# mLSTM cell and GELU feed-forward on one core: k and q of the later chunks copied into one piece in DRAM, their blocks loaded in 4 transfers

## The chip, the cores and the metric

One core of one Trainium2 chip. The metric is the time of one execution in device microseconds (us), as the median of several runs. Engines: PE (matrix multiply), PEld (its weight loads, which overlap PE), DVE (vector), ACT (activations), POOL (GpSimd), and SP, whose queue (SPq) issues every transfer of this kernel in program order.

## The reference

An mLSTM cell over batch 4, 8 heads, 768 steps and head size 40, and behind it a feed-forward layer on its output x (3072 tokens of 320 values).

```python
for t in range(S):
    m_new = np.maximum(f_gate[:, :, t] + m, i_gate[:, :, t])
    f_stab, i_stab = np.exp(f_gate[:, :, t] + m - m_new), np.exp(i_gate[:, :, t] - m_new)
    C = f_stab * C + i_stab * (v_t outer k_t);  n = f_stab * n + i_stab * k_t;  m = m_new
    y[:, :, t] = sigmoid(o_gate[:, :, t]) * (C q_t) / max(|n . q_t|, 1)
x = y.transpose(0, 2, 1, 3).reshape(3072, 320)
out = gelu(x @ moe_w_in) @ moe_w_out          # 320 -> 2048 -> 320
```

## The kernel before

The 768 steps are cut into 6 chunks of 128. Each chunk of each of the 4 batches is one unit n = 4c + b, in which the recurrence is written as matrix products: scores k times q for all heads, weighted by exponentials of the gates, times v, and a carried state per batch. After a chunk's cell comes its feed-forward part for 512 tokens: an upward product (`up`, three f32r products of high and low parts of x and of the weights, tiles `x_hi`, `x_lo`, `x_all`), GELU into the tile `g`, and a downward product in seven partial products (`down_steps`).

The program order is written by hand. `FRONT` plays the cells of chunks 0 and 1 and the unpacking of the weights. Then, for c = 1 to 5, `up` of chunk c is played, and after it the string `DOWN`, which mixes the downward products of chunk c (each `F` is one of 14 steps) with the cell of chunk c + 1. Inside `up`, the first two entries `K0 Q0` and `K1 Q1` of that next cell are already played. The letters that matter here, in the order of `DOWN` (`... F F`-steps between them left out): `M1 M0` masks on POOL; `L3` loads the blocks of the last batch; `S0 C0 h0` scores, state reads and state updates of batches 0 and 1; `B3` loads the gate rows of batch 3 into part of `g`; `K2 Q2 K3 Q3` transposes; `V0` ... `V3` values; `M2 M3` masks; `W3` exponentials; `D3` weighs v of batch 3 on POOL (tile `vw`, line 497); `S2 C2 h2` the same as `S0 C0 h0` for batches 2 and 3; `X`, `R` transposes and splits of x; `j` loads the blocks of the first batch of the chunk after.

For chunks 2 to 5, k and q come transposed. A block buffer has 128 partitions: row 64 i + d holds k (i = 0) or q (i = 1). `load_blocks` (lines 153 to 163, the transfer is line 160) fills it so that DVE's 32 by 32 transposes (line 458) give kT and qT: for k and q, for columns 0 to 31 and 32 to 39 of the head, and for 4 groups of 32 steps there is one transfer each, 16 per batch. Batches 0 to 2 of a chunk share one buffer (`blocks`), so each set is loaded after the transposes of the set before. Batch 3 uses half of `g`, the hidden tile of chunk c: `load_last` clears rows 32 to 63 and 96 to 127 on POOL (line 447) and loads 16 transfers, when the downward product no longer needs that part of `g`.

On SP's queue behind the 16 transfers of `L3` stand, in this order: the gate rows of batch 3 (line 177), k and v for batch 3 (line 148, four half transfers, which also wait until batch 0's k and v have been read), a `W` (line 180), k and v of the next unit (line 150). PE's state update of batches 2 and 3 (line 592) takes `vw` and `kb`.

Of the kernel before, what the change touches and what calls it, by code (L numbers as in the profile page):

```python
# [9 lines left out]
F32 = mybir.dt.float32  # L10
F32R = mybir.dt.float32r
# [5 lines left out]
P = 128  # L17
# [22 lines left out]
def kernel(  # L40
# [16 lines left out]
    nc = tc.nc  # L57

    B, H, S, D = q.shape
    L = P  # L60
    NCH = S // L
# [7 lines left out]
    TG = B * L  # L69
    R = P // 2  # L70
    NX = 2
# [12 lines left out]
    dram = ctx.enter_context(tc.tile_pool(name="dram", bufs=1, space=bass.MemoryType.DRAM))  # L84
# [36 lines left out]
    beyond = gates.tile([P, L], BF16, name="beyond")  # L121
    f_sb = gates.tile([BH, NCH, L], F32, name="f_sb")
    i_sb = gates.tile([BH, NCH, L], F32, name="i_sb")
    M_d = dram.tile([NCH - 1, BH, L], F32, name="M_d")
    swapped_d = [dram.tile([P, n, BH], F32, name=f"swapped{n}") for n in (NCH - 2, NCH - 3)]

# [12 lines left out]
    def load(n, first=0, end=4):  # L139
# [4 lines left out]
        for src, dst in ((q, qb), (k, kb), (v, vb), (o_gate, None))[first:end]:  # L144
            if dst and swapped(c, b):
                x, to = src[b, :, c * L:(c + 1) * L, :].rearrange("h p d -> p h d"), dst[turn_of(n)][:, :, 0:D]
                for i in range(2):
# [2 lines left out]
            nc.sync.dma_start(out=dst[turn_of(n)][:, :, 0:D] if dst else out_of(n),  # L150
                              in_=src[b, :, c * L:(c + 1) * L, :].rearrange("h p d -> p h d"))

    def load_blocks(n, to):

        c, b = divmod(n, B)
        for i, src in enumerate((k, q)):
            for d, w in ((0, 32), (32, D - 32)):
                for g in range(4):
                    t = c * L + 32 * g
                    nc.sync.dma_start(out=to[64 * i + d:64 * i + d + 32, :, 32 * g:32 * g + w],  # L160
                                      in_=src[b, :, t:t + 32, d:d + w].rearrange("h t d -> t h d"))
# [116 lines left out]
    def decays_last(g0, g1):  # L278
        g = slice(g0, g1)
        pd = ps_tr.tile([P, g1 - g0, BH], F32, name="pd", tag="tr")  # L280
        nc.tensor.matmul(pd.rearrange("p c n -> p (c n)"), last, gT[:, g].rearrange("p c n -> p (c n)"),
                         start=True, stop=True)
        by_half = pd.rearrange("p c (n two) -> p c n two", two=2)
        for hip in range(2):
            nc.vector.tensor_copy(out=dec[halves[hip], g], in_=by_half[halves[hip], :, :, hip])
# [109 lines left out]
    class Cell:  # L395
# [46 lines left out]

        def load_last(self, b):

            self.by_block = self.before.t[:, 0:HF, 0:P]
            for r in (32, 96):
                nc.gpsimd.memset(self.by_block[r:r + 32], 0.0)  # L447
            load_blocks(self.c * B + b, self.by_block)
# [14 lines left out]
        def turn_q(self, b):  # L463
            self.turn_half(b, 1)
            if b < B - 2:
                load_blocks(self.c * B + b + 1, by_block)
            if self.c < NCH - 1 and b < B - 1:
                self.weigh_values(b)
# [210 lines left out]

        def split_x(self, b):  # L680
            px, t = self.px.pop(b), slice(b * L, (b + 1) * L)
            hi = parts["x"][:, :, t]
            nc.vector.scalar_tensor_tensor(out=parts["x_lo"][:, :, t], in0=px, scalar=-1.0 / BASE, in1=hi, op0=OP.mult, op1=OP.add)
            nc.vector.tensor_tensor(out=parts["x_all"][:, :, t], in0=px, in1=hi, op=OP.subtract)


    HF, HT, HD = NF // 2, TG // 2, DM // 2
# [9 lines left out]
    w_sums, parts, fars, w_hi, w_lo, w_mid = [], {}, [], [], [], {}  # L697
    T = {1: lambda j: w_sums[0][:, j, :], 2: lambda j: w_sums[1][:, j, :], 3: Bm[0][1]}

    def products_begin():  # L700

        gate_ctx.close()
        pool = ctx.enter_context(tc.tile_pool(name="parts", bufs=1))
        w_sums.extend(pool.tile([P, HF, HD], F32, name=f"w_sums{n}") for n in range(2))
        for name in ("x_lo", "x_all"):
            parts[name] = pool.tile([P, NX + 1, TG], F32R, name=name)
        fars.extend([pool])

    def split_weight():
        i = len(w_lo)  # L710
        if i in (0, 3, 5, 8):
            two = shared([P, NX, 2, WP // 2], F32R, "w_in_hi")
            w_hi.extend([two[:, 0], two[:, 1]])
        elif i == 2:
            two = shared([P, 2, 2, WP // 2], F32R, "w_rest_hi")
            w_hi.append(two[:, 0])
            rest_two.append(two[:, 1])
        elif i == 7:
            w_hi.append(rest_two[0])
        w = w_all[i]  # L720
        nc.scalar.activation(out=w_hi[i], in_=w, func=AF.Copy, scale=PART * 2.0 ** -12)
        w_lo.append(w_f(F32R, "w_in_lo"))
        nc.vector.scalar_tensor_tensor(out=w_lo[i], in0=w_hi[i], scalar=-BASE * 2.0 ** 12, in1=w, op0=OP.mult, op1=OP.add)
# [3 lines left out]
    def join_weight(i):  # L727
        w_mid[i] = raw.tile([P, 2, WP // 2], F32R, name="w_in_mid", tag="pow") if i % 5 in (1, 4) else w_f(F32R, "w_mid")
        nc.vector.tensor_tensor(out=w_mid[i], in0=w_hi[i], in1=w_lo[i], op=OP.add)  # L729
# [22 lines left out]
    def hidden_sums(g, f0, f1):  # L752

        (a11, a21), (_, a22) = [[g.t[:, HF * e + f0:HF * e + f1, HT * h:HT * (h + 1)] for h in range(2)]
                                for e in range(2)]
        s1, s2 = [t[f0 // (HF // 2)][:, f0 % (HF // 2):f0 % (HF // 2) + f1 - f0, :] for t in (g.s1, g.s2)]
        nc.vector.tensor_tensor(out=s1, in0=a21, in1=a22, op=OP.add)  # L757
        nc.vector.tensor_tensor(out=s2, in0=s1, in1=a11, op=OP.subtract)
        nc.vector.tensor_tensor(out=a21, in0=a11, in1=a21, op=OP.subtract)  # L759
# [44 lines left out]
    def up(g, sums_too, turns):  # L804

        def split_to(i):
            while len(w_lo) <= i:
                split_weight()

        def pair(f, ahead):  # L810

            at = [f // 2 * 5 + f % 2 * 3 + x for x in range(NX)]
            split_to(at[1])
            for i in at:
                if i not in w_mid:
                    join_weight(i)
            pus = [[pool.tile([P, TG], F32, name="pu", tag=tag) for e in range(2)]
                   for pool, tag in (((ps_h, "h"), (ps_mm, "a")), ((ps_tr, "tr"), (ps_mm, "b")))[f % 2]]
            ahead()
            mid = [w_mid.pop(i) for i in at]  # L820
            for n, (w, x) in enumerate((([w_hi[i] for i in at], parts["x"]), ([w_lo[i] for i in at], parts["x_lo"]), (mid, parts["x_all"]))):
                for i in range(2):
                    for e in range(2):
                        for k in range(NX):
                            nc.tensor.matmul(pus[i][e], w[k][:, e, i * P:(i + 1) * P], x[:, k, :],  # L825
                                             start=(n == 0 and k == 0), stop=False, skip_group_check=True)
            return pus

        def rest(u, banks, order):
            mid = w_mid.pop(5 * u + 2)  # L830
            for i in order:
                pu = banks[i]
                for n, (w, x) in enumerate(((w_hi[5 * u + 2], parts["x"]), (w_lo[5 * u + 2], parts["x_lo"]), (mid, parts["x_all"]))):
                    for e in range(2):
                        r = halves[e]
                        nc.tensor.matmul(pu[e], w[r, i // 2, i % 2 * P:(i % 2 + 1) * P], x[r, NX, :], start=False,  # L836
                                         stop=(n == 2), skip_group_check=True)

        def out(i, e, pu):
            nc.scalar.activation(out=g.t[:, HF * e + i, :], in_=pu[e], func=AF.Gelu, scale=4097.0)  # L840

        b0 = pair(0, lambda: split_to(4))
        b1 = pair(1, lambda: join_weight(2))
        for step in turns[:1]:
            step()
        rest(0, b0 + b1, (0, 1, 2, 3))
        split_to(6)
        join_weight(5)
        join_weight(6)
        for i, pu in enumerate(b0 + b1):  # L850
            for e in range(2):
                out(i, e, pu)
        for step in sums_too[:5]:
            step()
        b2 = pair(2, lambda: split_to(9))
        hidden_sums(g, 0, 2)
        b3 = pair(3, lambda: (hidden_sums(g, 2, 4), join_weight(7)))
        for step in turns[1:] + sums_too[5:]:
            step()
        rest(1, b2 + b3, (2, 3, 0, 1))  # L860
        for i, e in ((2, 0), (2, 1), (3, 0), (0, 0), (1, 0), (3, 1), (0, 1), (1, 1)):
            out(4 + i, e, (b2 + b3)[i])
        hidden_sums(g, HF - 2, HF)
        hidden_sums(g, HF - 4, HF - 2)
# [100 lines left out]
    def cell_steps(c, letters, before=None):  # L965
# [11 lines left out]
                 d=lambda: decays_last(0, 1), q=lambda: decays_last(1, NCH - 1), r=halves_out, p=halves_back,  # L977
# [5 lines left out]
    for c in range(1, NCH):  # L983
        g, later, steps = Hidden(True), [], {}
# [38 lines left out]
```

## Time and profile before

| | |
|---|---|
| median of 3 runs | 488.13 us (486.6 to 488.46) |
| the profiled execution | 486.33 us, of which the span of the trace is 484.5 us |
| busy: PE / PEld / DVE / ACT / POOL | 471.9 / 408.0 / 338.0 / 244.0 / 76.7 us |
| PE's granted clock, mean | 0.996 |
| moved by DMA | 44.58 MB in 170429 packets, 156448 of them under 512 B |
| transfers issued on line 160 | 256 (192 into `blocks`, 64 into `g`) |
| loop c = 1 to 5: first matmul of `up` | about 129.4, 202.7, 278.7, 351.8 and 422.0 us |

The page comes from one execution, the traced one; its span and the 1.8 us around it make its own time. A stage's limit is read from the idle time of PE in that stage and from what ended it. "A <- B" names the instruction that waited and the one that came last before it.

### The profile page before, as it was taken

What the parts mean: (1) busy time and instruction counts of PE and PEld (TensorE: products, weight loads), DVE (VectorE), ACT (ScalarE), POOL (GpSimd) and SP (SyncE); (2) the same over time, 40 slices, a digit from 0 to 9 for tenths busy, and PEclk for the clock granted to TensorE, in tenths of its full rate; (3) what the DMA queues carried; (4) which work ended last, traced back from release to release, by engine and by line L of the source; (5) the groups of instructions that cost most, each with busy time, mean ns of one, the idle gap of its engine ahead of it and who ended that gap; (6) DMA issues with size and microseconds to landing.
All of it is one profiled execution on the core that took longest, in us unless ns stands there. A gap on an engine that the chain in (4) does not pass through costs nothing.

```text
span 484.5 us, 13245 instructions
## 1 busy us (share of the span) xinstructions
PE 471.9 (97%) x5380; PEld 408.0 (84%) x5380; DVE 338.0 (70%) x726; ACT 244.0 (50%) x521; POOL 76.7 (16%) x120
## 2 busy tenths in 40 slices
PE   8899999999999989999998999999999999999997
PEld 7787888777777979977988977888977899977997
DVE  7899699797879978656687555596755587624321
ACT  6977999844632953221963203774303784211300
POOL 3002200000020322500324500125400113100000
PEclk9999999999999999999998999999999999999999
DMA  9997955379320365651363751245751350100001
GB/s 178 189 226 175 220 138 147 90 190 213 105 29 8 38 136 108 112 107 13 33 141 77 127 106 17 34 87 130 136 107 17 33 95 4 38 20 0 1 1 54
DMA packets 170429, 44.58 MB, mean 92 GB/s; under 512 B 156448, under 2 KB 163904, under 8 KB 170368
## 3 DMA queue, kind: packets, MB, share of 16 engines
q1 hardware_dynamic: 170368, 43.73, 45.5%
q8 instruction: 42, 0.69, 0.6%
q14 instruction: 19, 0.16, 0.1%
HBM read 39.58 MB, written 4.13 MB: 90 GB/s over the span
## 4 chain that ended last, share of the span: by engine, by line
PE 67%; issue 12%; DVE 8%; SPq 4%; DMA 3%; ACT 2%; POOL 2%; DVEq 0%; POOLq 0%; ACTq 0%
PE po L900 22%; PE pu L825 16%; PE po L877 7%; PE pu L770 6%; PE pu L836 4%; PE ph L625 3%; SPq L160 2%; PE px L665 2%; PE pu L776 2%; PE ps L510 1%; SPq L150 1%; ACT g L840 1%; DMA g<-M_d 1%; DVE qT L458 1%; PE pf L548 1%
## 5 line engine op out<-in xcount | busy, mean ns | idle before, releaser
L840 ACT ACTIVATE g<-pu 128x512 f32<-128x512 f32 x80 | 40.8, 616 | 107.7 <-PE pu L836 107.6
L900 PE MATMUL po<-w_out,g 128*128 128x160 f32 x640 | 92.7, 301 | 0.0
L900 PEld LDWEIGHTS po<-w_out,g 128*128 128x128 f32 x640 | 87.9, 190 | 2.3 <-ACT g L840 1.8
L900 PE MATMUL po<-w_sums,sums 128*128 128x160 f32 x320 | 48.5, 309 | 0.0
L900 PEld LDWEIGHTS po<-w_sums,sums 128*128 128x128 f32 x320 | 45.4, 195 | 0.6
L825 PE MATMUL pu<-x_hi,w_in_hi 128*128 128x512 f32 x160 | 41.4, 400 | 0.0
L825 PE MATMUL pu<-x_lo,w_in_lo 128*128 128x512 f32 x160 | 40.6, 396 | 0.0
L435 ACT ACTIVATE W<-W,aT 128x128 f32<-128x128 f32 x128 | 38.7, 388 | 0.4
L825 PEld LDWEIGHTS pu<-x_hi,w_in_hi 128*128 128x128 f32 x160 | 29.4, 188 | 8.1 <-ACT g L840 1.9
L825 PEld LDWEIGHTS pu<-x_lo,w_in_lo 128*128 128x128 f32 x160 | 30.1, 188 | 7.2
L877 PE MATMUL po<-w_out,g 128*128 128x320 f32 x128 | 35.2, 433 | 0.0
L729 DVE TENSOR_TENSOR w_in_mid<-w_in_hi,w_in_lo 128x512 fp32r<-128x512 f32 x20 | 13.8, 688 | 29.5 <-PE pu L825 29.5
L877 PEld LDWEIGHTS po<-w_out,g 128*128 128x128 f32 x128 | 24.0, 190 | 9.6
L825 PE MATMUL pu<-x_all,w_mid 128*128 128x512 f32 x80 | 31.6, 395 | 0.0
L825 PE MATMUL pu<-x_all,w_in_mid 128*128 128x512 f32 x80 | 31.6, 395 | 0.0
L757 DVE TENSOR_TENSOR sums<-g 128x512 f32<-128x512 f32 x20 | 13.8, 688 | 25.5 <-ACT g L840 25.5
L913 DVE TENSOR_TENSOR o_sb<-po,o_sb 128x320 f32<-128x320 f32 (+1 forms) x27 | 12.5, 464 | 24.3 <-PE po L900 20.3
L409 POOL TENSOR_SCALAR_AFFINE_SELECT W<-W 128x1024 f32<-128x1024 f32 (+2 forms) x20 | 20.5, 1027 | 54.2 <-DMA W<-M_d 47.4
L770 PE MATMUL pu<-first_x,w_in 128*128 128x256 f32 x128 | 29.1, 382 | 0.0
L447 POOL MEMSET g<- 32x1024 f32 x8 | 7.6, 945 | 131.5 <-DVE g L759 94.9
L770 PEld LDWEIGHTS pu<-first_x,w_in 128*128 128x128 f32 x128 | 23.8, 190 | 3.5 <-DVE w_in L377 0.4
L532 DVE TENSOR_TENSOR W<-ps,W 128x256 f32<-128x256 f32 (+1 forms) x48 | 18.0, 415 | 11.1 <-PE ps L526 9.8
(185 smaller groups left out, 899.5 us busy)
## 6 DMA issues: line engine op xcount, KB each, us to landing
W<-M_d SPq DMA_DIRECT2D x16, 512.0 KB, 5.3
bits<-in_moe_w_in_dram SPq DMA_DIRECT2D x20, 256.0 KB, 4.4
bits<-in_moe_w_out_dram SPq DMA_DIRECT2D x16, 320.0 KB, 3.2
ob<-in_o_gate_dram SPq DMA_DIRECT2D x24, 160.0 KB, 4.0
out_dram<-o_sb SPq DMA_DIRECT2D x24, 160.0 KB, 1.9
vb<-in_v_dram SPq DMA_DIRECT2D x14, 160.0 KB, 5.2
kb<-in_k_dram SPq DMA_DIRECT2D x14, 160.0 KB, 4.9
g<-M_d SPq DMA_DIRECT2D x4, 512.0 KB, 4.8
```

Of the source, the lines that this page charges most:

```text
L409: nc.gpsimd.affine_select(out=x, in_=x, compare_op=OP.is_ge, fill=1.0e30, base=base, pattern=[[0, H], [1, x.shape[2]]], channel_multiplier=-1)
L435: nc.scalar.activation(out=W[n][:, h, :], in_=src, func=AF.Exp, scale=-1.0, bias=aT[:, self.c, r:r + 1])
L532: nc.vector.tensor_tensor(out=w[r, :, t], in0=ps[i][hip][r, :, t], in1=w[r, :, t], op=OP.mult)
L625: nc.tensor.matmul(ph[r, h, :], Pm[:, h, r], vb[turn_of(n)][:, h, :], start=True, stop=True)
L729: nc.vector.tensor_tensor(out=w_mid[i], in0=w_hi[i], in1=w_lo[i], op=OP.add)
L757: nc.vector.tensor_tensor(out=s1, in0=a21, in1=a22, op=OP.add)
L770: nc.tensor.matmul(banks[-1][e][:, i - i0, :], in_tile(i, x)[:, e, i % 2 * P:(i % 2 + 1) * P], first_x[:, x, t0:t1], start=(x == 0 and i = ...
L825: nc.tensor.matmul(pus[i][e], w[k][:, e, i * P:(i + 1) * P], x[:, k, :], start=(n == 0 and k == 0), stop=False, skip_group_check=True)
L836: nc.tensor.matmul(pu[e], w[r, i // 2, i % 2 * P:(i % 2 + 1) * P], x[r, NX, :], start=False, stop=(n == 2), skip_group_check=True)
L840: nc.scalar.activation(out=g.t[:, HF * e + i, :], in_=pu[e], func=AF.Gelu, scale=4097.0)
L877: nc.tensor.matmul(po[b], g.t[:, f, b * L:(b + 1) * L], w_out[:, f, :], start=(f == 0), stop=(f == NF - 1))
L900: nc.tensor.matmul(bank[at][:, i, :], lhs(j, t), rhs(j), start=(first and i == 0 and j == 0), stop=(i == n - 1 and j == HF - 1), skip_grou ...
```

## The change

- Eight DRAM tiles `kq_d` are added, for k and q of chunks 2 to 5, each of 4 batches x (8 heads x 128 steps) x 40 values. `copy_chunk` copies k and q of a chunk into them, DRAM to DRAM, one transfer of 160 KB for each batch and each of k and q, with rows of 1280 bytes.
- `copy_chunk(2)` stands at the start of `up` of c = 1 and copies batches 2 and 3 only (4 transfers). `copy_chunk(c + 2)` stands in `up` of c = 1, 2 and 3 after `K1 Q1` and copies all 4 batches (8 transfers).
- `load_blocks` of units n > 9 reads the copy. Heads and groups of steps are one dimension there, so a set takes 4 transfers instead of 16. Units 8 and 9 are loaded as before.
- The last batch's blocks no longer lie in `g` but in a tile `blocks3` that shares the buffer of `x_lo`. `x_lo` is made anew for each chunk at its first split.

```diff
+    kq_d = [[dram.tile([B, H * L, D], F32, name=f"{x}{c}_d") for x in "kq"] for c in range(2, NCH)]
...
+    def copy_chunk(c):
+
+        for b in range(B) if c > 2 else range(2, B):
+            for to, src in zip(kq_d[c - 2], (k, q)):
+                for x, y in ((src[b, :, c * L:(c + 1) * L, :], to[b]),):
+                    nc.sync.dma_start(out=y.rearrange("(h x t) d -> x h (t d)", h=H, x=16),
+                                        in_=x.rearrange("h (x t) d -> x h (t d)", x=16))
+
     def load_blocks(n, to):
...
             for d, w in ((0, 32), (32, D - 32)):
+                if n > 2 * B + 1:
+                    nc.sync.dma_start(out=to[64 * i + d:64 * i + d + 32].rearrange("t h (g w) -> t (h g) w", w=32)[:, :, 0:w],
+                                      in_=kq_d[c - 2][i][b, :, d:d + w].rearrange("(x t) d -> t x d", t=32))
+                    continue
                 for g in range(4):
...
         def load_last(self, b):
-            self.by_block = self.before.t[:, 0:HF, 0:P]
+            self.by_block = fars[0].tile([P, H, P], F32, name="blocks3", tag="x_lo", bufs=1)
...
         def split_x(self, b):
             px, t = self.px.pop(b), slice(b * L, (b + 1) * L)
+            if b == 0:
+                parts["x_lo"] = fars[0].tile([P, NX + 1, TG], F32R, name="x_lo", tag="x_lo", bufs=1)
...
-        for name in ("x_lo", "x_all"):
-            parts[name] = pool.tile([P, NX + 1, TG], F32R, name=name)
+        parts["x_all"] = pool.tile([P, NX + 1, TG], F32R, name="x_all")
...
+        if c == 1:
+            copy_chunk(2)
         b0 = pair(0, lambda: split_to(4))
...
         for step in turns[1:] + sums_too[5:]:
             step()
+        if c + 2 < NCH:
+            copy_chunk(c + 2)
         rest(1, b2 + b3, (2, 3, 0, 1))
```

## The prediction

> **What bounds the kernel now.** I read the page first, then PE's timeline around each `DOWN`, then for each gap the engine named as its releaser, and last SP's queue. The page says that PE is the bound:
>
> ```profile
> PE 471.9 (97%) x5380; PEld 408.0 (84%) x5380; DVE 338.0 (70%) x726; ACT 244.0 (50%) x521; POOL 76.7 (16%) x120
> ```
>
> The change does not touch a matmul, so it can only act through PE's 12.6 us of idle time (484.5 less 471.9), or through a slower clock after idle time. PE's timeline in the `DOWN` of c = 2 (start, length, instruction, then the idle time before it) has the largest piece:
>
> ```profile
> 253.37 0.51 PE L592 MATMUL pf<-vw,kb 128*40 128x41 f32 x16
> 254.55 0.31 PE L592 MATMUL pf<-vw,kb 128*40 128x41 f32 x5 [0.68 <-POOL vw L497]
> 256.18 0.52 PE L592 MATMUL pf<-vw,kb 128*40 128x41 f32 x11 [1.32 <-issue]
> 256.63 6.14 PE L900 MATMUL po<-w_sums,sums 128*128 128x160 f32 x32
> ```
>
> PE waits at `h2` for the weighed v of batch 3. The last line is 32 matmuls that take 4.61 us in the other chunks: 1.53 us more. The table by microsecond says why (the granted clock is the third number from the end):
>
> ```profile
> 256.00:257.00 1.00, 0.82 (x12) 0.74 (x13) 0.94 (x3) 0.00 (x0) 1.00 (x2) 0.68 0.04 8
> 258.00:259.00 1.00, 1.00 (x6) 1.00 (x5) 0.97 (x5) 0.98 (x2) 0.00 (x0) 0.50 0.00 0
> 260.00:261.00 1.00, 1.00 (x10) 1.00 (x9) 0.99 (x2) 0.09 (x1) 0.83 (x1) 1.00 0.00 0
> ```
>
> After the two gaps the clock is at half for some 3.4 us. What POOL waited for before that `vw`, and what SP's queue did then:
>
> ```profile
> 251.14 1.81 POOL L409 TENSOR_SCALAR_AFFINE_SELECT g<-g 64x1024 f32<-64x1024 f32 x2 [8.03 <-DMA g<-M_d]
> 253.76 0.73 POOL L497 TENSOR_TENSOR vw<-vb,ewT 128x328 f32<-128x328 f32 x1 [0.81 <-DMA vb<-in_v_dram]
> ```
> ```profile
> 236.72 4.82 SPq L160 DMA_DIRECT2D g<-in_k_dram  x8
> 241.58 5.06 SPq L160 DMA_DIRECT2D g<-in_q_dram  x8
> 246.74 0.40 SPq L177 DMA_DIRECT2D g<-M_d  x1
> 247.26 1.29 SPq L148 DMA_DIRECT2D kb<-in_k_dram  x2
> 248.95 1.27 SPq L148 DMA_DIRECT2D vb<-in_v_dram  x2
> ```
>
> SP spends 236.72 to 246.7 on the 16 transfers of `L3`; gate rows and v of batch 3 stand behind them. So issue time on SP reaches PE. The other `DOWN`s have the same gap, shorter: 0.87 us before line 592 at 330.75 (c = 3), 0.23 us at 181.65 (c = 1), none for c = 4, whose cell updates no state. c = 1 also has one wait for a block itself:
>
> ```profile
> 177.02 1.45 DVE L458 STREAM_TRANSPOSE qT<-g 64x512 f32<-64x512 f32 x2 [0.47 <-DMA g<-in_q_dram]
> ```
>
> **Removed issues.** Units 10 to 23 are 14 sets; 12 fewer transfers each make 168 issues at 0.449 us (the median of line 160's rows), 75 us of SP's queue. 28 copies at about 0.45 us put 12.6 us back. Most of this lies beside other work; what counts is `L3` (9.9 us in c = 2) and the set at `K1 Q1` before it (227.52 to 236.37).
>
> **Does a set also land faster?** The packets do not change: 4096 of 128 or 32 bytes. Between 211 and 221 us only one set runs, and the DMA share of its five 2 us rows is 0.26, 0.40, 0.38, 0.42, 0.15, together 3.2 us of full work for 7.7 us of issuing. So the DMA engines are under half used and the issue is the limit: 4 issues (1.8 to 2.4 us), 3.2 us on the DMA engines and the 2 us that a small transfer takes to land give 5 to 6 us instead of about 10. [...]
>
> **The copies.** No row shows a DRAM to DRAM transfer. Below: 160 KB at the 292 GB/s that the busiest microsecond shows (253 to 254) is 0.55 us of all 16 DMA engines. Above: the same bytes first read and then written, each at the 155 GB/s of a `W` (512 KB in 5.3 us of which 2 are landing), is 2.1 us. I take 0.8 us, near the lower end, since both sides have long rows like the weights' loads (2560 bytes, 283 GB/s between 104 and 108 us). They read inputs and write tiles that nobody holds, so they wait for nothing; each is used 20 us or more later. Behind them on SP stand only `L3` and what follows. `copy_chunk(2)` is 4 issues after 133 us, where SP's next transfer starts at 136.77 when DVE frees `blocks`; it costs nothing while 4 x 0.45 fits those 3.8 us, and 1 or 2 us of a block load with slack otherwise.
>
> **The new buffer.** `L3` waited for `g`, free after DVE's line 759 (236.57). It now waits for PE's last `x_lo` matmul, 231.25 by its row in `rest`. POOL's two memsets (1.95 us) go from 236.87 to about 231.3. Behind them on POOL is the state decay of `h0`, which waits for PE anyway. The `x_lo` written at `R0` must wait for the last transposes of `blocks3`; they are earlier on DVE itself, so this costs nothing.
>
> **The new schedule of c = 2**, from 227.52: 4 issues to 229.6, 8 copies to about 234, `L3` to about 236. `g` rows are free at 236.6, so the gate rows are issued at 236.6 instead of 246.74. The DMA engines have 3.2 + 8 x 0.8 + 3.2 = 12.8 us of work from 228 on, done at 241; the gate rows land by about 244, with `blocks3` at about 242, before DVE's `K3` at 247.5. k and v of batch 3 now wait for `V0`, whose matmuls end at 242.3: issued to 244.9, landed at about 249 (median 4.2 us), `vw` at 249.7. PE wants it at 253.9, so there are some 4 us of slack. c = 1 and c = 3 give the same by their own rows: `vw` at about 176 against 181.4, and at 326 against 329.9.
>
> **Sum.** c = 1: 0.47 + 0.23 = 0.7 us. c = 2: 0.68 + 1.32 + 1.53 = 3.5 us. c = 3: 0.87 us. Together 5.1 us, 486.33 to 481.2 for the profiled execution. The median stands 1.8 us above that one; 488.13 less 5.1 is 483.0. The doubtful part is the 1.32 us "issue": the trace names no cause, and it falls where the DMA share is 1.21 and 0.74. Its bounds are 0 (it stays, and the half clock with it: 2.85 us less gain) and the whole; I take the whole, since c = 1 and c = 3 run the same instructions without it. What stays: `S2` waits 0.31 us for DVE's transposes in c = 2 and 3, where DVE is busy without a break. The half clock follows two gaps of 2.0 us together, and I tie it to them. [...]
>
> **Rivals.** (1) Only the named waits go; the 1.32 us and the half clock stay or fall elsewhere, for the DMA engines are as full as before: 0.7 + 0.68 + 0.87 = 2.25 us, 485.9. For it: nothing in the trace ties them to `vw`. Against: the neighbouring chunks have neither. (2) Nothing reaches PE: gate rows and v come early, but DVE (no break from 237.65 to 250.9) and the next waits take the time back: 488. Against: after `h2` PE has two `F` steps ready, and c = 4, which lacks the wait, runs on with 0.18 us idle. (3) Slower, by the copies alone: they hold the DMA engines ahead of `L3`. `K3` at 247.5 is late once 229.6 + 8r + 3.2 + 2 passes 247.5, that is at r = 1.6 us a copy. At r = 2.1 it is 4.1 us late in three chunks, and the idle time brings the half clock, 1.5 us each: 3 x 5.6 = 17 us. The 5.1 us of waits on `vw` and the block would lie inside these, so 12 are new: 488 + 12 = 500. For it: no row shows such a transfer. Against: stores of 160 KB land in 1.9 us, so writing DRAM is quick.
>
> **How the numbers follow.** This kernel's runs differ by 0.4%, so 0.5% (2.4 us) is about what a measurement can tell from no change. Chances: the forecast 0.50 (482 to 485.5), rival 1 0.20 (485 to 487), rival 2 0.12 (487 to 489.5), rival 3 and its milder forms 0.18. Faster by over 0.5% (below 485.7): the forecast and a fifth of rival 1, 0.54. Same: 0.28. Slower: 0.18. The range goes from 481.5, somewhat under the forecast's sum, to 490.5, where the slow copies begin.
>
> **What would show it.** Right: line 160 has 88 transfers, the gate rows of c = 2 issue near 237, line 592 shows no wait on `vw` in c = 1 to 3, and the clock stays at 1.00 after 250 us. Wrong: copies that take over 1.6 us each, so that DVE's `K3` waits for `blocks3`; or PE's gaps of the same size at another line.

## The result, and the profile after

| | before | after |
|---|---|---|
| median | 488.29 us (486.6 to 490.11, 4 runs) | 480.66 us (479.91 to 481.03, 4 runs) |
| the profiled execution | 486.33 us, span 484.5 | 480.80 us, span 479.0 |
| PE's mean granted clock | 0.996 | 1.000 |
| busy PE | 471.9 us | 468.2 us |

The ratio is 0.9841, 95% interval 0.9803 to 0.9879. The change makes the kernel 7.6 us faster by the medians and 5.5 us by the two traced executions. The forecast was 483.0 us with a range from 481.5, so the result lies 0.8 us below the range.

From the page after, PE's busy time, and further down the queue that will matter in the last experiments (packets, MB, share of 16 DMA engines):

```profile
PE 468.2 (98%) x5380; PEld 405.0 (85%) x5380; DVE 338.9 (71%) x726; ACT 244.1 (51%) x521; POOL 78.3 (16%) x120
...
q8 instruction: 42, 0.69, 0.6%
```

SP's queue in the `DOWN` of c = 2 (start, length, transfer; line 159 is the copy, 168 the short block load, 190 the gate rows, 149 k and v of the last batch):

```profile
229.29 1.08 SPq L159 DMA_DIRECT2D k_d<-in_k_dram  x1
230.42 0.59 SPq L159 DMA_DIRECT2D q_d<-in_q_dram  x1
...
235.50 1.14 SPq L168 DMA_DIRECT2D blocks<-k_d  x2
236.69 1.65 SPq L168 DMA_DIRECT2D blocks<-q_d  x2
238.51 1.44 SPq L190 DMA_DIRECT2D g<-M_d  x1
240.62 1.32 SPq L149 DMA_DIRECT2D kb<-in_k_dram  x2
242.03 2.48 SPq L149 DMA_DIRECT2D vb<-in_v_dram  x2
```

`L3` now takes 235.50 to 238.3 instead of 236.72 to 246.7, and the gate rows are issued at 238.51 instead of 246.74. POOL follows, and so does PE (its timeline at `h2` of c = 2):

```profile
243.53 1.81 POOL L422 TENSOR_SCALAR_AFFINE_SELECT g<-g 64x1024 f32<-64x1024 f32 x2 [1.08 <-DMA g<-M_d]
246.65 0.74 POOL L510 TENSOR_TENSOR vw<-vb,ewT 128x328 f32<-128x328 f32 x1 [1.31 <-DMA vb<-in_v_dram]
```
```profile
252.71 0.61 PE L605 MATMUL pf<-vw,kb 128*40 128x41 f32 x21
253.87 0.43 PE L605 MATMUL pf<-vw,kb 128*40 128x41 f32 x11 [0.55 <-issue]
254.23 4.61 PE L918 MATMUL po<-w_sums,sums 128*128 128x160 f32 x32
```

`vw` of batch 3 is ready at 247.4, PE wants it at 253.2, and no `h2` waits for it any more. The 32 matmuls behind `h2` take 4.61 us (6.14 before) at a granted clock of 1.00, so the half clock is gone too. One piece stays: an idle time of 0.55 us that the trace gives no releaser for ("issue"), behind the same 21st matmul of 32 as before. The DMA engines are done earlier too, at 250 instead of 255.8 (share of the 16 engines next to last; the kernel before has 1.21 and 0.74 in 254 to 256):

```profile
249.00:250.00 1.00, 1.00 (x9) 0.43 (x7) 0.97 (x2) 0.67 (x2) 0.00 (x0) 1.00 0.96 101
250.00:251.00 1.00, 0.69 (x33) 0.69 (x34) 0.26 (x1) 1.00 (x1) 0.00 (x0) 1.00 0.02 4
```

The loops, from the first matmul of one `up` to the next, show where the 5.5 us lie:

| | start to c = 1 | c = 1 | c = 2 | c = 3 | c = 4 | c = 5 |
|---|---|---|---|---|---|---|
| before | 128.95 | 73.74 | 76.03 | 73.05 | 70.19 | 62.57 |
| after | 129.20 | 72.85 | 72.74 | 71.95 | 69.70 | 62.54 |
| gained | -0.25 | 0.89 | 3.29 | 1.10 | 0.49 | 0.03 |
| predicted | 0 | 0.70 | 3.53 | 0.87 | 0 | 0 |

(The first `up` of the kernel before starts at 128.95; the "about 129.4" of the table ahead of the prediction is 0.45 us late.)

### The profile page after: what moved, and what is told of

Same layout as the page of the kernel before. It is cut to its first block, busy times and chain, and to the rows that moved or that the text cites. A ratio compares the mean times of both kernels' runs of the same rounds, so it can differ in the third digit from the quotient of the medians.

```text
span 479.0 us, 13005 instructions
## 1 busy us (share of the span) xinstructions
PE 468.2 (98%) x5380; PEld 405.0 (85%) x5380; DVE 338.9 (71%) x726; ACT 244.1 (51%) x521; POOL 78.3 (16%) x120
## 4 chain that ended last, share of the span: by engine, by line
PE 82%; DVE 8%; DMA 5%; SPq 2%; issue 1%; ACT 1%; POOL 0%; DVEq 0%; POOLq 0%
PE po L918 27%; PE pu L839 22%; PE po L895 7%; PE pu L784 6%; PE pu L850 6%; PE ph L638 3%; PE ps L539 2%; DVE qT L471 2%; PE px L678 2%; PE pu L790 2%; DMA g<-M_d 2%; PE pf L594 1%; DVE kT L471 1%; PE ps L523 1%; SPq L151 1%
## 5 line engine op out<-in xcount | busy, mean ns | idle before, releaser
L918 PE MATMUL po<-w_sums,sums 128*128 128x160 f32 x320 | 47.0, 303 | 0.0
L918 PEld LDWEIGHTS po<-w_sums,sums 128*128 128x128 f32 x320 | 43.9, 190 | 0.6
L422 POOL TENSOR_SCALAR_AFFINE_SELECT W<-W 128x1024 f32<-128x1024 f32 (+2 forms) x20 | 21.5, 1078 | 54.6 <-DMA W<-M_d 47.9
L667 ACT COPY y_rest<-ob 128x128 f32<-128x128 f32 x16 | 4.8, 298 | 40.7 <-DVE ob L660 38.7
L460 POOL MEMSET blocks<- 32x1024 f32 x8 | 7.6, 945 | 108.5 <-PE pu L850 108.3
```

Of the source, the lines that this page charges most:

```text
L422: nc.gpsimd.affine_select(out=x, in_=x, compare_op=OP.is_ge, fill=1.0e30, base=base, pattern=[[0, H], [1, x.shape[2]]], channel_multiplier=-1)
L918: nc.tensor.matmul(bank[at][:, i, :], lhs(j, t), rhs(j), start=(first and i == 0 and j == 0), stop=(i == n - 1 and j == HF - 1), skip_grou ...
```

## The experiments

**How much the kernel before differs from itself.** `e1_before_again` is the kernel before, unchanged.

> The kernel before, unchanged, to see how its executions differ. The traced execution of before (486.33 us) lost 5.5 us to that of after, the medians 7.6. Theory A: the executions of before differ by their count of half-clock stretches of about 3.4 us, each 1.5 to 1.7 us long in time and 0.0035 in the mean granted clock; so the times spread from 486 to 490 and the longer ones show the lower clock (0.993 or less against 0.996). Rival B: the waits of PE for v of batch 3 differ in length from one execution to the next, as transfers land earlier or later; then the times spread as much, the clock stays the same, and a second trace shows the gaps of line 592 at other lengths with one half-clock stretch or none.

Measured: 488.85 us median (485.42 to 490.89), ratio 0.9999 (0.9964 to 1.0035). The spread goes with the clock: executions with a mean clock of 1.000 took 485.4 to 488.6 us, those at 0.992 or 0.993 took 489.5 to 490.9. The clock is not all of it: at 1.000 they still differ by 3.2 us, as the rival has it. Over all 78 executions of the kernel before that have their clock on record, 12 of `e1` and 66 beside the other runs (the stretch of half clock in the trace of the kernel before is 3.41 us long, and one of that length lowers the mean by 0.0035):

| half-clock stretches, from the mean clock | 0 | 1 | 2 | 3 | 4 | 5 |
|---|---|---|---|---|---|---|
| executions | 17 | 30 | 19 | 9 | 2 | 1 |
| median, us | 486.3 | 488.8 | 489.9 | 490.8 | 493.7 | 492.0 |

A straight line through all of them rises by 1.5 us for each stretch. The trace of `e1` has the waits of the one before, but another split at c = 2:

```profile
255.86 0.31 PE L592 MATMUL pf<-vw,kb 128*40 128x41 f32 x5 [0.34 <-POOL vw L497]
258.36 0.43 PE L592 MATMUL pf<-vw,kb 128*40 128x41 f32 x11 [2.20 <-issue]
```

So the traced execution of the kernel before, with one stretch and 486.33 us, was faster than all 30 with one stretch in the table (486.6 to 491.3); it is not a plain offset below the median.

**Which part of the change does it.** Three kernels have one part each. `e2_buffer_only` is the kernel before with the last batch's blocks in the buffer of `x_lo`, still in 16 transfers and without copies:

```diff
-            self.by_block = self.before.t[:, 0:HF, 0:P]
+            self.by_block = fars[0].tile([P, H, P], F32, name="blocks3", tag="x_lo", bufs=1)
```

> Only the second part of the change: the last batch's blocks lie in the buffer of x_lo, and every set is still loaded with 16 transfers from the inputs, with no copies. The queue of SP reaches the set of the last batch at 236.4 instead of 236.7 in the second loop, 163.0 instead of 164.2 in the first, 311.3 instead of 312.7 in the third. Theory: issue time on SP is what counts, so the gate rows and v of batch 3 come only 0.3 to 1.4 us earlier: 0.3 to 0.9 us less wait in loops 1 and 3, the half clock of loop 2 stays; 1 to 2 us faster than before, 486 to 487. Rival: the wait for g is what held the set back, and the new buffer alone gives most of the gain: 482 to 483.

Measured: 487.27 us (485.52 to 489.42), ratio 0.9967 (0.9935 to 0.9999). That is 1.5 us less than the kernel before beside it (488.77), the size that the theory gave, though the interval all but reaches 1. In its trace the only half-clock stretch lies at 15 us and none in c = 2, and at `h2` of c = 2 PE has no wait on `vw` at all, but a longer unnamed gap:

```profile
255.56 0.61 PE L592 MATMUL pf<-vw,kb 128*40 128x41 f32 x21
258.99 0.43 PE L592 MATMUL pf<-vw,kb 128*40 128x41 f32 x11 [2.82 <-issue]
```

`e3_copies_rest` has the copies and the short loads for batches 0 to 2, but batch 3 stays in `g` with 16 transfers:

```diff
-                if n > 2 * B + 1:
+                if n > 2 * B + 1 and b < B - 1:
```

> The copies and the 4-transfer loads for batches 0 to 2 alone; the last batch's blocks stay in g and are loaded with 16 transfers from the inputs. Theory: the set of the last batch still starts when g is free (236.6 in the second loop) and still takes 9 to 10 us of SP, so gate rows and v of batch 3 come as in before, and the copies are only work that nobody waits for: 487 to 489, no change. Rival: the issue time saved on the other sets is worth something by itself (sends, gates, the next k and v come earlier): 484 to 486.

Measured: 489.53 us (488.09 to 491.08), ratio 1.0008 (0.998 to 1.0036), mean clock 0.989 to 0.996. It saves 120 of the 168 issues and gains nothing. SP's queue and PE at c = 2, where again no wait on `vw` is left, and the unnamed gap is the longest of all:

```profile
237.63 4.88 SPq L173 DMA_DIRECT2D g<-in_k_dram  x8
242.56 4.91 SPq L173 DMA_DIRECT2D g<-in_q_dram  x8
247.56 0.40 SPq L190 DMA_DIRECT2D g<-M_d  x1
```
```profile
254.28 0.69 PE L605 MATMUL pf<-vw,kb 128*40 128x41 f32 x21
258.68 0.64 PE L605 MATMUL pf<-vw,kb 128*40 128x41 f32 x11 [3.72 <-issue]
```

`e4_last_only` is the opposite: only batch 3's k and q are copied (8 copies instead of 28) and loaded in 4 transfers into the new buffer, all others in 16.

```diff
-        for b in range(B) if c > 2 else range(2, B):
+        for b in range(B - 1, B):
...
-                if n > 2 * B + 1:
+                if n > 2 * B + 1 and b == B - 1:
```

> The complement: only the last batch's blocks come from a copy, with 4 transfers, into the buffer of x_lo; only that batch's k and q are copied (2 copies a chunk), and batches 0 to 2 are loaded with 16 transfers as in before. Theory: the set of the last batch is all that stands before the gate rows and v of batch 3; it runs from 236.4 to about 238.7, v of batch 3 lands at about 248, and PE does not wait for it: 481 to 482, nearly the whole gain of 7.6 us. Rival: the set at Q1 before it (227.5 to 236.4) has to shrink too: 484 to 486.

Measured: 480.68 us (480.39 to 480.96), ratio 0.9831 (0.9791 to 0.9872), mean clock 0.999 or 1.000: the whole change, to 0.02 us. SP's queue:

```profile
236.73 1.15 SPq L168 DMA_DIRECT2D blocks<-k_d  x2
237.93 2.65 SPq L168 DMA_DIRECT2D blocks<-q_d  x2
240.75 0.61 SPq L190 DMA_DIRECT2D g<-M_d  x1
```

What counts is the set that stands ahead of the gate rows, as the prediction had it; the other sets lie beside other work. The other copies alone give nothing and the buffer alone 1.5 us; the short set without the new buffer was not run.

**What a copy costs.** `e5_double_copies` is the kernel after with each copy sent twice, the second time to a spare tile.

```diff
-                for x, y in ((src[b, :, c * L:(c + 1) * L, :], to[b]),):
+                for x, y in ((src[b, :, c * L:(c + 1) * L, :], to[b]), (src[b, :, c * L:(c + 1) * L, :], also[b])):
```

> The changed kernel with every copy sent twice, the second into spare DRAM tiles that nobody reads: 28 more copies, 8 more in front of each set of the last batch. By the trace of the changed kernel a copy takes 0.60 us of SP and some 0.7 us of the 16 DMA engines, so in the second loop the set of the last batch starts 4.8 us later (about 240.3) and v of batch 3 is weighed at about 252 instead of 246.65, PE wants it at 253.2. Theory: the slack of about 6 us pays for nearly all of it: 480.7 to 482.5, no half clock in most executions. Rival (copies are dear, and the change lives on the edge): a wait on vw of 1 us or more comes back in three loops, with half-clock stretches: 485 to 489.

Measured: 487.22 us (483.18 to 489.45), ratio 0.9971 (0.9937 to 1.0005), mean clock 0.992 to 1.0. My expectation fell; the time is the rival's, but the waits on `vw` are 0.6 us in c = 1 and c = 2 and none in c = 3, not 1 us in each. The second set of copies takes nearly all of the gain back; in the traces, 3.8 of the 4.2 us that it costs lie in c = 2. SP, POOL and PE at c = 2:

```profile
241.27 1.22 SPq L169 DMA_DIRECT2D blocks<-k_d  x2
...
245.75 0.44 SPq L191 DMA_DIRECT2D g<-M_d  x1
```
```profile
253.18 0.73 POOL L511 TENSOR_TENSOR vw<-vb,ewT 128x328 f32<-128x328 f32 x1 [0.87 <-DMA vb<-in_v_dram]
```
```profile
253.96 0.31 PE L606 MATMUL pf<-vw,kb 128*40 128x41 f32 x5 [0.59 <-POOL vw L511]
256.20 0.43 PE L606 MATMUL pf<-vw,kb 128*40 128x41 f32 x11 [1.93 <-issue]
```

In the trace of the kernel after, a copy costs 0.60 us of SP's queue (the median issue) and lands in 3.1 us. Eight more push `L3` from 235.50 to 241.27 and the gate rows from 238.51 to 245.75; `vw` is ready at 253.9 instead of 247.4, past the 253.4 at which PE wants it. It is the same queue that the change relieved, and what it left there is under 6.5 us of room. The unnamed gap of 1.93 us and the half clock behind it weigh more than the wait of 0.59 us; the run adds issue time and traffic together and does not part them.

**A step earlier for DVE.** The 0.31 us before `S2` is a wait for DVE's transposes. `e6_q3_early` moves `Q3` right behind `K3` in the string `DOWN`.

> A version meant to beat both: the changed kernel with Q3 (transposes of q of batch 3) played right behind K3, ahead of F M3 G0 V1 F W3. On DVE they then go ahead of the 0.5 us addition of V1. What is left of PE's waits in the changed kernel is S2 behind these transposes in loops 1 to 3 (0.31 us named idle time each, about 0.9 us in all by when the 56 matmuls start). Theory: DVE has no break there, so 0.5 us come off each of three loops: 479.0 to 479.5. Rival: q's block of batch 3 has not landed yet or the addition of V1 is now late for the product behind it, and nothing changes: 480.4 to 481.

Measured: 480.09 us (479.71 to 480.87), ratio 0.9834 (0.9796 to 0.9871). Expectation missed. The wait has a new owner, and `S2` starts no earlier in its loop:

```profile
249.72 1.45 PE L539 MATMUL ps<-qT,kT 64*64 64x128 f32 x56 [0.63 <-DVE far L646]
```

It stands 0.6 us below the kernel after by the medians and 0.7 us by the traces, and 0.5 of these lie ahead of the first `up` (128.69 against 129.20), where the edit acts on nothing that I can name. Its interval holds the kernel after, so it isn't shown to be faster; no run here beats the kernel after by more than that.

**The unnamed gap and the DMA engines.** `e7_extra_load` is the kernel after with 8 useless transfers of 160 KB in each chunk behind k and v, from 247.25 to 255.8 on SP; `vw` is ready as early as before.

> The changed kernel with 8 more transfers per chunk that nobody waits for, 160 KB each in packets of 160 bytes, DRAM to DRAM, issued behind V1's loads (about 247 in the second loop), so that the DMA engines stay full until about 254. v of batch 3 has landed by then, so no wait on vw can come from it. In all five traces PE stops after 21 of the 32 matmuls of h2 in the second loop, with no named releaser: 2.0 us (two gaps), 2.5, 2.8 and 3.7 where the DMA engines were full until 255.8 to 257, and 0.55 and 0.48 where they were idle from 250. Theory: this gap depends on the load of the DMA engines and not on vw; it grows to 1.3 us or more, half-clock stretches come back in part of the executions: 482 to 485. Rival: the gap follows the wait on vw; it stays at 0.55 us, 480.4 to 481.3.

Measured: 481.47 us (481.17 to 485.37), ratio 0.9876 (0.9827 to 0.9925). With nothing but DMA traffic added, the gap grows from 0.55 to 1.48 us, and one of four executions fell to a mean clock of 0.992. The gap is the theory's (1.3 us or more); the median lies between the two expectations:

```profile
254.65 0.42 PE L606 MATMUL pf<-vw,kb 128*40 128x41 f32 x11 [1.48 <-issue]
```

`e8_shifted` is the kernel before with 10 tiny float32 products at PE's start, to see whether the gap belongs to a place in PE's stream.

> The kernel before with 10 tiny matmuls (32 by 32) added at its start, where PE waits for the gates anyway. Everything behind them is unchanged but stands 10 matmuls later in PE's stream. Theory: the gap without a releaser in h2 of the second loop belongs to a place in PE's instruction stream, so it moves from behind matmul 21 of 32 to behind matmul 11, whatever the times are; the total is as before, 486 to 491. Rival: it belongs to a certain operand of h2 and stays behind matmul 21.

Measured: 486.83 us, one execution, clock 0.995. The gap behind matmul 21 is gone, but nothing stands at matmul 11 either; the expectation's place was miscounted, since each of these float32 products is two matmuls in the trace (the 32 of `e12`, below, are 64). Every gap over 0.3 us of c = 2 now has a name, and the wait on `vw` is about as long as both gaps of the kernel before together (2.00 us):

```profile
255.49 0.78 PE L595 MATMUL pf<-vw,kb 128*40 128x41 f32 x16 [2.17 <-POOL vw L500]
```

**The half clock without any transfer.** `e9_late_vw_10` and `e10_late_vw_12` are the kernel after with the last batch's `vw` computed 10 and 12 times in a row on POOL, so that PE waits while the DMA engines are as idle as in the kernel after.

```diff
+            for _ in range(12 if self.c > 1 and b == B - 1 else 1):
```

> The kernel after, in which POOL computes the weighed v of the last batch 10 times in a row in each loop (the last one counts), so that it is ready about 1 to 2 us after PE wants it at the second set of h2 (one takes 0.74 us, the first begins at 246.65 in c = 2, PE is there at 253.2). No transfer is added, and the DMA engines stay as idle as in the kernel after. Theory A (idle time of PE alone brings the half clock): a wait on vw of 0.5 to 2 us in each of c = 1, 2 and 3, 2 to 6 us in all, 482.5 to 486.5 us, mean clock below 0.999 in several executions. Theory B (the half clock needs the unnamed gap that comes with busy DMA engines): the same waits, 482.5 to 486 us, the mean clock 0.999 or above in all executions.

> As the run before, with 12 repetitions: the wait on vw is 1.5 to 1.7 us longer in each of the three loops, 2 to 3.5 us each. Theory A: 487 to 494 us, with one half-clock stretch (1.7 us) or more in most executions, mean clock 0.990 to 0.997. Theory B: 486.5 to 490 us, mean clock 0.999 or above, and executions that agree within 1 us.

Measured: 493.25 us (median of all ten, 487.83 to 496.74, clock 0.982 to 0.996) with 10, and 499.37 us (497.56 to 501.49, clock 0.976 to 0.990) with 12. The waits came out longer than meant, but A against B is settled for these kernels: idle time of PE (1.62 to 3.64 us at a time with 10) is enough. With 10, PE's timeline at c = 1, 2 and 3, and the table by microsecond behind two of the waits (granted clock third from the end):

```profile
184.58 0.51 PE L606 MATMUL pf<-vw,kb 128*40 128x41 f32 x16 [3.64 <-POOL vw L511]
...
260.20 0.51 PE L606 MATMUL pf<-vw,kb 128*40 128x41 f32 x16 [1.79 <-POOL vw L511]
...
335.65 0.69 PE L606 MATMUL pf<-vw,kb 128*40 128x41 f32 x16 [1.62 <-POOL vw L511]
```
```profile
261.00:262.00 1.00, 1.00 (x5) 1.00 (x5) 0.81 (x2) 0.02 (x1) 1.00 (x3) 0.50 0.00 0
336.00:337.00 1.00, 1.00 (x13) 0.92 (x10) 0.49 (x2) 0.00 (x0) 1.00 (x3) 0.50 0.00 0
```

Each wait is followed by one stretch of 3.41 us at half clock. They start at 185.62, 260.71 and 335.80 by the clock record of the trace: 75.09 us apart, which is 22 times 3.413, both times. With 12 the waits are 4.85, 2.86 and 3.60 us, the stretches 6.8 us, and they start 78.51 and 78.50 us apart, 23 times 3.413. `e1` has the same: stretches at 180.36 and 258.87, 78.51 us apart. In the trace of the kernel before, by its clock record, the clock is full for 249.173 us, half for 3.413 and full for 225.280, which are 73, 1 and 66 times 3.4133; in that of the kernel after it is full for 474.453 us, 139 times 3.4133. So in these traces the clock changes on a grid of 3.413 us, though the loops of the kernel before, 73.74, 76.03 and 73.05 us, are no multiples of it. I laid this grid over the nine traces that have a stretch (those of the last two experiments too) and read PE's busy share in each of its windows in the `DOWN`s. All fifteen windows at full clock in which PE was busy for 0.54 or less (0.12 to 0.54) were followed by half clock, and so was one of 0.64; the other windows, five of them between 0.58 and 0.69, were not. My estimate from these counts: a gap of some 1.6 us (0.46 of 3.41) in one of these `DOWN`s brings a half window if it falls into one window, and can pass without one if it lies across two. That would make the same wait cost 1.7 us, half of 3.41, in one execution and nothing in the next. Not every stretch belongs to `h2`: `e2` and `e10` have one at 15 us, ahead of everything that the change touches, `e1` and `e3` one in c = 1, where PE waits for DVE's transposes of batch 3, and `e12` one in c = 4 behind a wait of 2.32 us for DVE.

**Filling the wait.** `e11_filled` is the kernel before with 8 useless 128 x 128 products ahead of the last `h2` set.

```diff
+                    for _ in range(8 if b == B - 1 else 0):
+                        nc.tensor.matmul(banks[1][:, H:H + NP, :].rearrange("p h d -> p (h d)")[:, 0:P], ident, ident,
+                                         start=True, stop=True, skip_group_check=True)
```

> The kernel before, in which PE computes 8 useless 128 x 128 products ahead of the second set of h2 in c = 0 to 4 (0.1 to 0.2 us each, 0.9 us or so in all, of which the part in the waits on vw of c = 1 to 3 costs nothing). They shorten the idle time there and leave the transfers as they are. Theory (the spread of the kernel before comes from idle time at h2 and the half clock behind it): fewer half-clock stretches than in the kernel before, mean clock 0.997 or above in most executions, median 487 to 489.5 us, within 1 us of the kernel before, and less spread. Rival (the stretches have to do with something else than the length of the idle time, such as the unnamed gap): as many stretches as before, 489 to 492 us.

Measured: 493.32 us (489.67 to 496.78), ratio 1.0074 (1.0031 to 1.0117); both expectations missed, for the fill takes 2.05 us in each of three loops (16 matmuls in the trace) and not 0.9, more than the waits that it covers in c = 1 and c = 3. Four of ten executions ran at clock 1.000, the others at 0.993 to 0.997. The traced one has full clock, no wait on `vw`, and new unnamed gaps of 1.19 and 0.83 us in c = 3 and c = 4. Where the stretches of the others lie isn't shown.

**What the unnamed gap is.** Counting PE's matmuls in the trace up to each unnamed gap of the runs so far gave 1107 (0.33 to 0.77 us at 93 us, in most kernels), 2885 (c = 2), and 3901 and 4792 (`e11`). Their distances are 14, 8 and 7 times 127, the last one 2 over. `e12_shift_64` is the kernel before with 32 of the tiny products of `e8` at the start.

> The kernel before with 32 tiny float32 products at its start, 64 matmuls in the trace, which lie partly in PE's first waits; 486 to 493 us. In the traces so far PE's unnamed gaps stand before its recorded matmuls number 1107, 2885, 3901 and 4792, whose distances are 14, 8 and 7 times 127, and the page lists a queue for instructions with 42 pieces of 16.4 KB, which is the 2 x 5380 matmuls and weight loads by 256 of 64 bytes. Theory (PE waits for the next piece of its own program): any unnamed gap of over 0.3 us stands before a matmul whose number is 1107 plus a multiple of 127, within 3, so none at matmul 21 of the 32 of c = 2, whose number is now 2949. Rival (something about these operands or these places of the schedule): the gaps at matmul 21 in c = 2 or after 56 of the 64 values at 93 us are there again, or new ones stand at numbers off that lattice.

Measured: 495.94 us, one execution, clock 0.986 (the kernel before beside it 492.01). Both old gaps are gone, and two new ones stand at other places:

```profile
181.85 0.35 PE L595 MATMUL pf<-vw,kb 128*40 128x41 f32 x8 [0.37 <-issue]
```
```profile
330.84 0.23 PE L595 MATMUL pf<-vw,kb 128*40 128x41 f32 x1 [1.16 <-POOL vw L500]
333.16 0.77 PE L595 MATMUL pf<-vw,kb 128*40 128x41 f32 x15 [2.08 <-issue]
```

Their matmuls are number 1996 and 3901: 1107 plus 7 and plus 22 times 127, to the unit. So in these kernels the gap belongs to a fixed spacing in PE's own stream, not to an operand or to a step of the schedule. The spacing fits the queue q8 that the pages call "instruction": it has 42 transfers, PE has 10760 matmuls and weight loads, 256.2 for each transfer, and 127 of each make 254. The 64 bytes of the expectation are the same division, an estimate: 16,384 bytes by 256.2.

The kept traces also hold the transfers of that queue, 16,384 bytes each, one for each of these places; `e11` and `e12`, with 96 and 128 PE instructions more, have 43 of them. At matmul 2885 (us from the start of the span):

| trace | PE passes the place before (matmul 2758) | transfer starts | ends | PE goes on | unnamed gap |
|---|---|---|---|---|---|
| before | 251.36 | 253.74 | 254.67 | 256.18 | 1.32 |
| `e3` | 252.27 | 256.13 | 257.39 | 258.68 | 3.72 |
| `e7` | 250.55 | 251.84 | 253.10 | 254.65 | 1.48 |
| after | 250.70 | 251.35 | 252.50 | 253.87 | 0.55 |
| `e8` | 249.48 | 249.81 | 250.82 | 252.82 | none |

Over all fourteen traces there are 26 unnamed gaps of over 0.1 us (0.15 to 3.72 us), all at these places or within 2 matmuls of them, and at each of them PE goes on 1.2 to 1.6 us after the transfer has ended. At the other 550 places PE arrives 1.46 us or more after its end and does not stop. I read this as PE waiting there for the next piece of its own program; no view names the transfer as the releaser. At the gaps, the transfer starts 0.7 to 1.3 us after PE has passed the place before where the DMA engines are idle or half used, and 1.1 to 3.9 us after where they are full. By these numbers a gap shows where PE goes through the 127 matmuls in less time than this start, the transfer (0.9 to 1.4 us) and the 1.2 to 1.6 us behind it take together: PE needs 2.9 us for them at 93 us, where the engines are idle (a share of 0.00 from 91 to 94 in the kernel before), and 2.5 to 3.5 us at `h2` of c = 2.

## Why the prediction was right and where it was wrong

- **The mechanism held for the queue, and only in part for the wait.** Issue time on SP ahead of the gate rows was the cause: `e4` alone gives all of it, `e2` 1.5 us and `e3` nothing. The sum of 5.1 us stands against 5.5 us between the two traced executions, and "486.33 to 481.2 for the profiled execution" against 480.80. But the prediction let all of c = 2 hang on `vw`. There the wait that ended last was the one at the place in PE's stream, as I read it for the next piece of its program: in the kernel before, by the table of the transfers, it would have held PE until 256.18 however early `vw` was, and `e2` and `e3` lose 2.82 and 3.72 us to it without any wait on `vw`. Where no such place falls into `h2` (`e8`), `vw` alone held PE for 2.17 us. The change removes both, for the shorter set also lets the DMA engines finish at 250 and not at 255.8.
- **The step that failed** is "The median stands 1.8 us above that one; 488.13 less 5.1 is 483.0". It carried the difference between the traced execution and the median over to the new kernel as a constant. That difference is made mostly of what the change removes: 0 to 5 half-clock stretches at about 1.5 us, and gaps of varying length. The kernel after has the clock at 1.000 in all four executions and a median (480.66) at its traced time (480.80). The median therefore gained 7.6 us, not 5.1: 2.1 of the missing 2.5 us are this offset (1.96 us before, -0.14 after), and 0.4 are terms of the sum. The low end of the range should have started below 481.2, the sum without that offset. That the traced sum came within 0.4 us is in part luck: the terms missed by -0.25 to 0.49 us each, and in `e1`'s trace the same loops c = 1 to 4 stand 8.8 us above the kernel after.
- **The half clock.** The prediction tied it to the two gaps of 2.0 us together, and `e9` and `e10` bear out that idle time of that length is enough: 1.62 us before the last stretch of `e9`. What the prediction did not have is the grid of 3.413 us; a window with PE busy for 0.54 was enough.
- **The 1.32 us "issue"** was taken whole, "since c = 1 and c = 3 run the same instructions without it"; 0.55 us of it stayed, so c = 2 gave 3.29 and not 3.53. That reason fails: the gap goes by the place in PE's stream. It shrank with the DMA engines done 6 us earlier, and it grows again with added traffic and `vw` as early as ever (`e7`, 1.48 us), or when the loads slip (`e5`, 1.93 us). At 550 of 576 places in the traces PE did not stop; at the others it was 0.15 to 3.72 us.
- **The copies.** They were put at 0.45 us of SP each ("to about 234"); they take 0.60, two of the eight over 1 us, and `L3` began at 235.50. The 0.8 us of DMA work was harmless, and rival 3's price of 1.6 us isn't reached; but `e5` shows a way to a slower kernel that no rival had, by SP's queue and the traffic behind it.
- **The set in 4 transfers.** 2.8 us of issuing in place of 9.9, against the 2 us assumed; the gate rows were issued at 238.51 and not 236.6. Both slips did no harm, for v of batch 3 landed by 246.65 and not at about 249; the slack, put at "some 4 us", measured 5.8 (247.4 to 253.2). The 2 us for a small transfer to land is what the kernel before shows for the parts of its sets (medians of 2.0 to 2.3); those of the short set took 2.4 to 3.0.
- **Small terms.** c = 3 gave 1.10 for 0.87, and c = 4 gave 0.49 where the sum has nothing. A term was left out there: before its first transposes of x, PE waits for DVE in c = 4, by 0.18 us in the trace of the kernel before, 1.27 in `e1`, and 0.45, 0.48, 0.83 and 2.32 in `e2`, `e3`, `e8` and `e12`; of the traces with the long set for batch 3 only `e11` is without this wait, and no trace with the short set has it. That points to `L3` reaching PE in c = 4 too, though its cell updates no state; by which links was not followed, and what the rest of the 0.49 us is stays open. The first part lost 0.25 us; other traces start the first `up` anywhere from 128.2 to 130.7, so I make nothing of it.
- Rivals 1 and 2 kept the waits or moved them; neither happened. Rival 1's reason was right, though: the 1.32 us does go with the load of the DMA engines, only that load ended earlier as well. DVE's break-free stretch that spoke for rival 2 is seen in `e6`, where it takes back a step moved forward.

## What to carry to other kernels

When the kernel's executions differ by more than the change is worth, ask what the difference is made of before carrying it over: if the change removes its cause, forecast the median from the sum on a trace without stalls, not from the old median. In one queue that issues everything, look for the set that stands ahead of the late load and shorten that one alone; here 8 copies do what 28 do. In these runs stalls of 1.62 and 1.79 us on PE (`e9`) had a stretch of half clock behind them, and one of 1.48 us (`e7`, clock 1.000) had none. A stretch cost 1.5 us by the line through the executions, at most 1.7 us (half of 3.41): price such a stall with it as a chance and not a certainty.

## What the runs showed of the hardware that I had not expected

- In these traces the granted clock changed on a grid of 3.413 us (starts 22 and 23 windows apart to 0.02 us in `e9`, `e10` and `e1`; stretches of 73, 1, 66 and 139 windows in the kernels before and after). All fifteen windows at full clock with PE busy 0.54 or less, in the `DOWN`s of nine traces, were followed by one at half; in two cases of `e10` a window at half with PE busy for 0.74 to 0.80 was followed by another at half.
- In fourteen traces PE stopped 26 times for 0.15 to 3.72 us at places 127 pairs of matmul and weight load apart, until 1.2 to 1.6 us after a 16 KB transfer of the queue "instruction" had ended. This queue moved 0.69 MB in 42 transfers for a kernel with 10760 matmuls and weight loads, and with the DMA engines full such a transfer started up to 3.9 us after PE had passed the place before.
- In the trace of the kernel after, a DRAM to DRAM transfer of 160 KB in rows of 1280 bytes took 0.60 us to issue and landed in 3.1 us (medians of 28), and eight in a row took 6.1 us to issue, with the DMA engines busy for 0.80 of the time (229.3 to 236).
